# Attention kernel, last ten units: PV ten slots behind to the end, sums turned by DMA up to unit 125, closing tiles finished one after the other, tail loads spread over six units

## The chip, the cores and the metric

The kernel runs on one core of one Trainium2 chip. A core has five engines that run side by side, each with its own instruction stream in fixed order: TensorE (PE, matrix products into PSUM), VectorE (DVE), ScalarE (ACT, here the exponentials), GpSimd (POOL) and SyncE (SP). DMAs are issued from the streams of SP, POOL and ACT. The metric is the device time of one execution in microseconds (us); lower is better. Three runs of the kernel before gave 1253.02, 1253.81 and 1254.78 us; the median is 1253.81.

## The reference

Sizes: 2048 tokens, D = 512, 32 heads of 128, 2048 cached keys, MLP width 1792. All inputs are bf16. `mixer_mlp` stands for the second branch, a token mixer and an MLP with two GELUs.

```
def _A_ref(x, k_cache, v_cache, wq, wo):
    q = (x @ wq).reshape(B, Sq, H, Dh).transpose(0, 2, 1, 3)
    scores = einsum("bhqd,bhkd->bhqk", q, k_cache) * (Dh ** -0.5)
    p = softmax(scores, axis=-1)
    o = einsum("bhqk,bhkd->bhqd", p, v_cache)
    return o.transpose(0, 2, 1, 3).reshape(B, Sq, H * Dh) @ wo

xn = layernorm(x)
s = _A_ref(xn, k_cache, v_cache, wq, wo)
g = silu(mixer_mlp(xn, w1, w2, w3, w4))
return x + s * g
```

## The kernel before, in words

**Units and slots.** The attention is cut into 128 units (`units`, L130): 8 groups of 4 heads, in each group 4 query tiles of 512 tokens, in each of these the 4 heads. A unit has 8 slots, p0 to p7, 1024 slots in all (the loop of L791). In each slot PE forms the scores of 256 keys (`s_slot`, 2 matmuls into one of two PSUM buffers `ps_s`), ACT takes the exponential into `pT` (L207, 128x1024), and PE multiplies earlier exponentials with the values (`pv_slot`, 2 matmuls into `ps_o`, two buffers). How many slots PV runs behind the scores is read from the list `LAGS` (L137): 5 at the start, 10 from the middle of unit 6 on, and between unit 120 and p2 of unit 122 back to 5, one at a time, so that five slots there hold two PV pairs.

**Other work in the slots.** PE also forms the next queries (`q_mm`, 4 matmuls in p0 and p1 of a unit, none in the last two units), the products with `wo` for one tile of 128 tokens (`wo_mm`, p4 and p5; DVE adds the result to `s_acc` in p6, `wo_post`) and the matmuls of the second branch (`ps_m`, p2, p3, p6, p7), which end in unit 120. Of the two single PSUM buffers, `xa` and `xm`, `wo` uses `xa` and the second branch `xm`.

**The sum of the softmax.** DVE adds the exponentials of a unit (`add_first`, `add_next`, `fold`) to one tile of 128x512; what is left is a sum over the 128 partitions. There are two ways. For *turned* units (`turned`, L249: units 4 to 117, `T1` = 118) SP issues a DMA transpose of the tile into `accT` (`acc_turn`, p3 of the next unit), DVE reduces it (`turned_sums`, L260, at p0 of the unit after that), takes the reciprocal (L245), SP writes it to DRAM (`dr`) and reads it back spread over all partitions (`rb`, `bcast`, p2), and DVE normalises `ps_o` with it into `oT` (`norm`, L287, p7, two units later). There is one buffer `accT` and one `rb`. For the other units PE forms the sum with 4 matmuls on a column of ones (`sums`, L240, p3 of the next unit), the rest is the same, `bcast` comes one slot later and `norm` (L294) at p2 of the unit after.

**The end.** `QUIET` is unit 121. The products of the last two query tiles with the heads of group 6 are deferred: their `oT` goes to DRAM (`o_d`) and is loaded back as `oS` by `tail_open` at the start of unit 121, with the gates `gf` and inputs `xf` of token tiles 12 to 15 (10 loads in one place of the program). Tiles 8 to 11 belong to query tile 2 of the last group; the loop finishes 8, 9 and 10, each with 4 matmuls on `oS` and 4 on `oT`. DVE writes each out (`wo_out`, p3 of the next unit). `gate_sum` (L332, L334) prepares the sums of tiles 12 to 15. After the loop (L888 on) come the sum of unit 127 in three pieces (`split_sums`, 40 small matmuls), its last five PV slots, tile 11, then tiles 12 to 15: the parts that need only heads 0 to 2 first, then `norm` of unit 127 in two halves, then head 3 of tiles 12 and 13, tile 14, and tile 15 in two halves. `last_scale` (L338, DVE) and `last_out` (L343, on POOL for tiles 12 and 13, on DVE for the rest) end each tile.

Of the kernel before, what the change touches and what calls it, by code (L numbers as in the profile page):

```python
# [10 lines left out]
FP32 = mybir.dt.float32  # L11
BF16 = mybir.dt.bfloat16
# [5 lines left out]
def kernel(  # L18
# [15 lines left out]
    nc = tc.nc  # L34
# [9 lines left out]
    NT = Sq // P  # L44
# [180 lines left out]
    def pv_slot(u, p):  # L225
        g, qt, hh = units[u]
        s = st[u]
        if p == 0:
            s["o"] = psO.tile([P, 512], FP32, name="ps_o")
        pT = s["pT"][p // 2]  # L230
        for j in range(2):
            kc = 2 * p + j
            mm(s["o"][:], vBs[g * HG + hh][:, kc, :], pT[:, 2 * (p % 2) + j, :], kc == 0, kc == KC - 1)

    def sums(u):
        s = st[u]
        ps = psX.tile([P, 4], FP32, tag="xm" if u + 1 == QUIET - 1 else "xa", name="ps_sum")
# [11 lines left out]
    def turned(u):  # L249
        return T0 <= u < T1  # L250
# [22 lines left out]
            recip(s, s["ps"])  # L273

    def bcast(u):
        st[u]["rb"] = rp.tile([P, 512], FP32, name="rb")
        pin(nc.sync.dma_start(
            out=st[u]["rb"][:], in_=st[u]["dr"][:].rearrange("a b -> (a b)").partition_broadcast(P)))

    def norm(u, pieces=1):  # L280
        g, qt, hh = units[u]
        s = st.pop(u)
        if hh == 0:
            oTs[(g, qt)] = otp.tile([P, HG, 512], BF16, name="oT")
        if turned(u):
            f = "x (j p) -> x j p"
            pin(nc.vector.tensor_tensor(  # L287
                out=oTs[(g, qt)][:, hh, :].rearrange(f, j=4), in0=s["o"].rearrange(f, j=4),
                in1=s["rb"].rearrange("x (p j) -> x j p", j=4), op=ALU.mult))
            return  # L290
        w = 512 // pieces
        for i in range(pieces):
            c = slice(i * w, (i + 1) * w)
            pin(nc.vector.tensor_tensor(  # L294
                out=oTs[(g, qt)][:, hh, c], in0=s["o"][:, c], in1=s["rb"][:, c], op=ALU.mult))

    wo_box = {}

    def wo_mm(g, t, hhs, tag="xa"):
        if hhs[0] == 0:  # L300
            wo_box[0] = psX.tile([P, D], FP32, tag=tag, name="ps_wo")
        held = g == NG - 1 and (NG - 2, t // 4) in deferred
        if held and hhs[0] == 0:
            wo_part(wo_box[0][:], g - 1, t, range(HG), True, False)
        wo_part(wo_box[0][:], g, t, hhs, hhs[0] == 0 and not held, hhs[-1] == HG - 1)
# [10 lines left out]
    def tail_open():  # L316
        ph.close()
        ph3 = ph.enter_context(pool("ph3", reuse_waits="tile"))
        for g, qt in deferred:
            oTs[(g, qt)] = ph3.tile([P, HG, 512], BF16, name=f"oS{qt}")  # L320
            pin(nc.sync.dma_start(out=oTs[(g, qt)][:], in_=o_d[qt][:]))
        for t in range(4 * LQ, NT):
            gf = ph3.tile([P, D], BF16, name=f"gf{t}")
            pin(nc.sync.dma_start(out=gf[:], in_=g_d[t][:]))
            xf = ph3.tile([P, D], BF16, name=f"xf{t}")
            pin(nc.sync.dma_start(out=xf[:], in_=xsrc[t]))
            tl[t] = (gf, xf)

    def gate_sum(t):
        gf, xf = tl[t]  # L330
# [10 lines left out]
    def last_out(t, eng, cs=slice(0, D), queue=nc.sync):  # L341
        gf, xf = tl[t]
        pin(eng.tensor_tensor(out=xf[:, cs], in0=gf[:, cs], in1=s_acc[:, t, cs], op=ALU.add))  # L343
        pin(queue.dma_start(out=out2d[t * P:(t + 1) * P, cs], in_=xf[:, cs]))
# [10 lines left out]
    def wo_post(g, t):  # L355
        ps = wo_box.pop(0)
        sa = s_acc[:, t, :]
        if g == 0:
            pin(nc.vector.tensor_copy(out=sa, in_=ps[:]))
            return  # L360
        pin(nc.vector.tensor_tensor(out=sa, in0=ps[:], in1=sa, op=ALU.add))  # L361

    def wo_out(t):
        sa = s_acc[:, t, :]
        xl, gl = fin.pop(t)
        pin(nc.vector.scalar_tensor_tensor(
            out=gl[:], in0=sa, scalar=0.5, in1=gl[:], op0=ALU.mult, op1=ALU.mult))
        pin(nc.vector.tensor_tensor(out=xl[:], in0=gl[:], in1=xl[:], op=ALU.add))
        pin(nc.sync.dma_start(out=out2d[t * P:(t + 1) * P, :], in_=xl[:]))
# [421 lines left out]
    for n in range(NS):  # L791
# [33 lines left out]
            acc_turn(u - 1)  # L825
        if p == 2 and u >= 2 and turned(u - 2):
            bcast(u - 2)
        if p == (4 if u == T1 + 2 else 2) and u >= 2 and not turned(u - 2):
            normed(u - 2)
        if p == 3 and u >= 1 and not turned(u - 1):  # L830
            sums(u - 1)
        if p == 4 and u >= 1 and u != T1 + 1 and not turned(u - 1):
# [12 lines left out]
        if u == QUIET - 1 and p >= 6:  # L845
            wo_mm(*wo_todo[0], (0, 1) if p == 6 else (2, 3), "xm")
            if p == 7:
                gg, t = wo_todo.popleft()
                wo_post(gg, t)
                at(n + 5, lambda t=t: wo_out(t))  # L850
        if p == 4:
            add_first(u)
        if p == 4 and u == NU - 1:
# [37 lines left out]
    assert min(todo) >= NS and not chunks and len(wo_todo) == 1  # L891
    U = NU - 1
    GL = NG - 1
    s = st[U]
    gg, t11 = wo_todo.popleft()
    ts = [4 * LQ + j for j in range(4)]
    norm(U - 1)
    held = range(HG)
    ready = range(HG - 1)
    pv_slot(U, 3)  # L900
    split_sums(U, [(s["acc"][:, i, :], i == 0, False) for i in range(2)]
               + [(s["pT"][2][:, i, :], False, False) for i in range(4)])
    pv_slot(U, 4)
    split_sums(U, [(s["pT"][3][:, i, :], False, False) for i in range(2)])
    pv_slot(U, 5)
    split_sums(U, [(s["pT"][3][:, i, :], False, i == 3) for i in range(2, 4)])
    bcast(U)
    for fn in late:
        fn()
    for t in ts[2:]:  # L910
        gate_sum(t)
    pv_slot(U, 6)
    pv_slot(U, 7)
    wo_mm(gg, t11, (0, 1, 2, 3))
    wo_post(gg, t11)
    wo_out(t11)
# [5 lines left out]
    for j in (0, 1):  # L922
        wo_part(dst[j], GL - 1, ts[j], held, True, False)
        wo_part(dst[j], GL, ts[j], ready, False, False)
    wo_part(dst[2], GL - 1, ts[2], held, True, False)
    norm(U, 2)
    for j in (0, 1):
        wo_part(dst[j], GL, ts[j], (HG - 1,), False, True)
        last_scale(ts[j], dst[j])
        last_out(ts[j], nc.gpsimd)  # L930
    wo_part(dst[2], GL, ts[2], range(HG), False, True)
    last_scale(ts[2], dst[2])
    last_out(ts[2], nc.vector)
    for i, queue in enumerate((nc.sync, nc.scalar)):
        cs = slice(i * D // 2, (i + 1) * D // 2)
        ps = halves[i][:, cs]
        wo_part(ps, GL - 1, ts[3], held, True, False, cs)
# [34 lines left out]
```

## Time and profile before

| | |
|---|---|
| time, median of 3 runs | 1253.81 us |
| the profiled execution: its time | 1253.69 us |
| its span in the trace | 1251.9 us |
| PE / DVE / ACT / POOL busy | 1242.8 / 1107.5 / 1130.6 / 139.5 us |
| exponentials (L207) | 1024 of 1028 ns mean |
| DMA moved | 126.70 MB |

The span is counted from the first to the last record of the profiled execution; the rest of its time, 1.8 us, lies around it. Times in the profile are microseconds from the start of the span. A matmul's record holds its passage through the array, so records of matmuls that follow each other overlap, and the distance of their starts is what one costs; the same holds, less so, for DVE. L123 is the helper that issues every matmul, so PE work is told apart by the tile it writes. PEld is the load of a matmul's weights, which overlaps the matmul before. In square brackets a row shows how long the engine sat idle before it and what ended that.

### The profile page before, as it was taken

The page shows a single profiled execution, that of the slowest core. Times are in us where ns is not written, and L with a number is a line of the kernel's source. Part 1 is how long each engine was busy: PE and PEld are TensorE (multiplying, and loading weights), DVE is VectorE, ACT ScalarE, POOL GpSimd, SP SyncE. Part 2 cuts the span into 40 slices and gives each one's busy share as a digit, 9 for nine tenths or more (in the row PEclk, how much of TensorE's full clock was granted, in tenths as well). Part 3 has the DMA queues.
Part 4 walks back from the last instruction along what each step waited for, and adds up shares of the span by engine and source line. Part 5 has one row for each costly group of instructions (what it writes and reads, how often), then busy time and mean ns, then how long its engine had stood idle before and what let it go on. Part 6 is the DMA issues. An engine that isn't in the chain of part 4 may idle for free.

```text
span 1251.9 us, 16586 instructions
## 1 busy us (share of the span) xinstructions
PE 1242.8 (99%) x5872; PEld 599.1 (48%) x5872; DVE 1107.5 (88%) x1509; ACT 1130.6 (90%) x1285; POOL 139.5 (11%) x239
## 2 busy tenths in 40 slices
PE   9999999999999999999999999999999999999998
PEld 5444444444444444444444444444444444444444
DVE  7899999999899988899988889999888999888887
ACT  7999998888999888899988889998888999988893
POOL 4410003332101000000100000010000000000111
PEclk9999999999999999999999999999999999999999
DMA  9654444565635555344663345554535343564532
GB/s 185 136 114 88 78 106 80 118 149 109 135 72 114 118 95 102 61 91 90 111 126 76 69 93 97 110 71 108 97 89 108 66 89 81 115 134 74 154 72 69
DMA packets 235108, 126.70 MB, mean 101 GB/s; under 512 B 186832, under 2 KB 212048, under 8 KB 235024
## 3 DMA queue, kind: packets, MB, share of 16 engines
q1 hardware_dynamic: 225920, 100.40, 41.8%
q0 software_dynamic: 8672, 24.91, 7.9%
q8 instruction: 46, 0.75, 0.3%
q14 instruction: 38, 0.31, 0.1%
q10 hardware_dynamic: 432, 0.33, 0.1%
HBM read 82.58 MB, written 7.60 MB: 72 GB/s over the span
## 4 chain that ended last, share of the span: by engine, by line
PE 96%; DMA 1%; ACT 1%; DVE 1%; issue 0%; SPq 0%; POOL 0%; POOLq 0%; DVEq 0%
PE ps_s L123 35%; PE ps_o L123 34%; PE ps_m L123 10%; PE ps_q L123 9%; PE ps_wo L123 8%; ACT pT L207 1%; DMA dr<-rc 1%; DMA w_sb<-in_B_w_dram 0%; DMA rb<-dr 0%; PE ps_sum L123 0%; DVE gf L338 0%; DVE xf L343 0%; ACT pre L528 0%; DVE qT L193 0%; DVE bn L384 0%
## 5 line engine op out<-in xcount | busy, mean ns | idle before, releaser
L207 ACT ACTIVATE pT<-ps_s 128x1024 bf16<-128x1024 f32 x1024 | 1024.4, 1028 | 99.2 <-PE ps_s L123 88.7
L123 PE MATMUL ps_s<-qT,kT 128*128 128x512 bf16 x2048 | 608.9, 379 | 0.9 <-ACT pT L207 0.5
L123 PE MATMUL ps_o<-pT,vb 128*128 128x512 bf16 x2048 | 608.0, 379 | 0.3 <-DVE oT L294 0.3
L123 PEld LDWEIGHTS <-kT 128*128 128x128 bf16 x2048 | 231.1, 113 | 226.1 <-issue 4.9
L218 DVE TENSOR_TENSOR acc<-acc,pT 128x2048 bf16<-128x2048 bf16 x254 | 306.4, 1206 | 10.1 <-ACT pT L207 9.9
L123 PEld LDWEIGHTS <-vb 128*128 128x128 bf16 x2048 | 200.0, 98 | 225.8 <-DMA vb<-in_A_v_cache_dram 0.5
L213 DVE TENSOR_TENSOR acc<-pT 128x2048 bf16<-128x2048 bf16 x128 | 156.2, 1220 | 31.8 <-ACT pT L207 31.6
L123 PE MATMUL ps_q<-xnT,wq_h 128*128 128x512 bf16 (+1 forms) x524 | 152.8, 374 | 0.8 <-ACT xnT L459 0.6
L123 PE MATMUL ps_wo<-wo_h,oT 128*128 128x512 bf16 (+1 forms) x476 | 140.2, 377 | 0.2 <-DVE qT L193 0.2
L287 DVE TENSOR_TENSOR oT<-ps_o,rb 128x512 bf16<-128x512 f32 x114 | 122.3, 1073 | 8.9 <-DMA rb<-dr 8.9
L361 DVE TENSOR_TENSOR s_acc<-ps_wo,s_acc 128x512 f32<-128x512 f32 x100 | 68.7, 687 | 43.5 <-PE ps_wo L123 43.2
L222 DVE TENSOR_TENSOR acc<-acc 128x1024 bf16<-128x1024 bf16 x127 | 86.8, 683 | 0.9
L193 DVE CAST qT<-ps_q 128x512 bf16<-128x512 f32 x109 | 74.9, 688 | 8.7 <-PE ps_q L123 7.7
L123 PEld LDWEIGHTS <-wq_h 128*128 128x128 bf16 x524 | 50.8, 98 | 61.1 <-issue 1.3
L260 DVE TENSOR_REDUCE sm<-accT 128x4 f32<-128x512 bf16 x114 | 77.5, 680 | 0.5 <-DMA accT<-acc 0.2
L123 PE MATMUL ps_m<-xn2T,w_sb 128*128 128x512 bf16 x224 | 77.1, 379 | 0.0
L123 PE MATMUL ps_m<-w_sb,h2T 128*128 128x512 bf16 x224 | 77.1, 379 | 0.0
L123 PEld LDWEIGHTS <-oT 128*128 128x128 bf16 x484 | 47.3, 98 | 57.6 <-DVE oT L294 1.4
L659 POOL DMA_DIRECT2D w_sb<-in_B_w_dram x28 | 21.1, 754 | 370.4 <-PE ps_m L123 370.4
L687 POOL DMA_DIRECT2D g_d<-xr x16 | 8.7, 546 | 442.3 <-DVE xr L685 376.5
L223 DVE TENSOR_TENSOR acc<-acc 128x512 bf16<-128x512 bf16 x127 | 54.0, 425 | 4.4
L496 DVE SCALAR_TENSOR_TENSOR sq<-sq,pre 128x1024 bf16<-128x1024 bf16 x36 | 44.0, 1221 | 3.9 <-ACT sq L492 3.9
(89 smaller groups left out, 602.9 us busy)
## 6 DMA issues: line engine op xcount, KB each, us to landing
rb<-dr SPq DMA_DIRECT2D x128, 256.0 KB, 4.2
vb<-in_A_v_cache_dram SPq DMA_DIRECT2D x64, 256.0 KB, 3.6
w_sb<-in_B_w_dram POOLq DMA_DIRECT2D x28, 256.0 KB, 3.8
wo_h<-in_A_wo_dram SPq DMA_DIRECT2D x32, 128.0 KB, 3.0
wq_h<-in_A_wq_dram SPq DMA_DIRECT2D x28, 128.0 KB, 3.1
kT<-in_A_k_cache_dram SPq DMA_TRANSPOSE x128, 3.4
dr<-rc SPq DMA_DIRECT2D x128, 2.0 KB, 1.6
xr<-in_A_x_dram POOLq DMA_DIRECT2D x16, 128.0 KB, 2.5
```

The lines of the kernel that those rows point to most:

```text
L123: pin(nc.tensor.matmul(out=out, lhsT=lhsT, rhs=rhs, start=start, stop=stop))
L193: pin(nc.vector.tensor_copy(out=qT[:], in_=st[u].pop("psq")[:]))
L207: pin(nc.scalar.activation(out=s["pT"][-1][:, jj:jj + 2, :], in_=sps[:], func=ACT.Exp, scale=SCALE))
L213: pin(nc.vector.tensor_tensor(out=s["acc"][:], in0=s["pT"][0][:], in1=s["pT"][1][:], op=ALU.add))
L218: pin(nc.vector.tensor_tensor(out=a[:], in0=a[:], in1=st[u]["pT"][i][:], op=ALU.add))
L222: pin(nc.vector.tensor_tensor(out=a[:, 0:2, :], in0=a[:, 0:2, :], in1=a[:, 2:4, :], op=ALU.add))
L223: pin(nc.vector.tensor_tensor(out=a[:, 0, :], in0=a[:, 0, :], in1=a[:, 1, :], op=ALU.add))
L260: pin(nc.vector.tensor_reduce(out=sm[:], in_=s.pop("at")[:], axis=mybir.AxisListType.X, op=ALU.add))
L287: pin(nc.vector.tensor_tensor(out=oTs[(g, qt)][:, hh, :].rearrange(f, j=4), in0=s["o"].rearrange(f, j=4), in1=s["rb"].rearrange("x (p j) - ...
L361: pin(nc.vector.tensor_tensor(out=sa, in0=ps[:], in1=sa, op=ALU.add))
L496: pin(nc.vector.scalar_tensor_tensor(out=sq[:].rearrange(f2), in0=sq[:].rearrange(f2), scalar=1.0, in1=pre[:].rearrange(f2), op0=ALU.add, ...
L659: pin(nc.gpsimd.dma_start(out=w[:], in_=w3_v[:, :, fc * P:(fc + 2) * P]))
```

## The change

- `LAGS` no longer goes down: PV stays 10 slots behind to the end, so 10 PV slots are left after the loop instead of 5 (6 and 7 of unit 126, all of 127).
- `T1` is 126: units 118 to 125 are turned too, 126 and 127 are summed on PE. In unit 127 `sums` and `bcast` of unit 126 come one slot later than before. The special places of `bcast` and `normed` around the old `T1` go. `rb` of units 126 and 127 gets two buffers of its own.
- The loads of the tail are issued one group per unit at p5 of units 121 to 126, in the order: `gf`, `xf` of tile 12; of 13; `oS` of query tile 2; `gf`, `xf` of 14; `oS` of 3; `gf`, `xf` of 15.
- The wo products: `normed` of unit 123 now falls in p7 of unit 125, so tile 8 is done in unit 126, tile 9 in 127 (their parts on `oS` in p2 and p3, on `oT` in p4 and p5, in `xm`); tiles 10 and 11 are left for after the loop. The second wo tile of unit 120 (`QUIET` - 1, p6 and p7) goes; tiles 3 to 7 are then done one per unit in 121 to 125.
- After the loop: the sums of unit 127, with PV slots 6 and 7 of unit 126 between them, then tile 10, the eight PV slots of unit 127, tile 11, then tiles 12, 13, 14 whole, each with its scale and its add, and 15 in halves. All adds of `last_out` are on DVE.

```diff
-    T0, T1 = 4, NU - 10
-    LAGS = [(T0 * SPU + 4 * (i + 1), LAG + i) for i in range(5)] + [((T1 + 2) * SPU + 2, LAG + 5)]
-    LAGS += [((T1 + 2) * SPU + 6 + 4 * i, LAG + 4 - i) for i in range(4)] + [(NS, LAG)]
+    T0, T1 = 4, NU - 2
+    LAGS = [(T0 * SPU + 4 * (i + 1), LAG + i) for i in range(5)] + [(NS, LAG + 5)]
...
-        st[u]["rb"] = rp.tile([P, 512], FP32, name="rb")
+        st[u]["rb"] = (tl["rb"].tile([P, 512], FP32, tag="rb3", bufs=2, name="rb") if u >= T1 else rp.tile([P, 512], FP32, name="rb"))
...
+    def held_load(g, qt):
+        pin(nc.sync.dma_start(out=oTs[(g, qt)][:], in_=o_d[qt][:]))
+
+    def gate_load(t):
+        for tile_, src in zip(tl[t], (g_d[t][:], xsrc[t])):
+            pin(nc.sync.dma_start(out=tile_[:], in_=src))
...
+    loads = [lambda t=t: gate_load(t) for t in range(4 * LQ, NT)]
+    for i, (g, qt) in enumerate(deferred):
+        loads.insert(2 + 2 * i, lambda g=g, qt=qt: held_load(g, qt))
+    for i, load in enumerate(loads):
+        at((QUIET + i) * SPU + 5, load)
...
-        if p == 3 and u >= 1 and not turned(u - 1):
+        if p == (4 if u > T1 else 3) and u >= 1 and not turned(u - 1):
             sums(u - 1)
...
         if p in (4, 5) and wo_todo:
-            wo_mm(*wo_todo[0], (0, 1) if p == 4 else (2, 3))
+            wo_mm(*wo_todo[0], (0, 1) if p == 4 else (2, 3), "xm" if u >= NU - 2 else "xa")
+        if p in (2, 3) and u >= NU - 2:
+            wo_held(*wo_todo[0], (0, 1) if p == 2 else (2, 3))
...
+    split_sums(U, [(a, i == 0, False) for i, a in enumerate(acc + pT2)])
+    pv_slot(U - 1, 6)
+    split_sums(U, [(a, False, False) for a in pT3[:2]])
+    pv_slot(U - 1, 7)
+    split_sums(U, [(a, False, i == 1) for i, a in enumerate(pT3[2:])])
     bcast(U)
     for fn in late:
         fn()
     for t in ts[2:]:
         gate_sum(t)
+    norm(U - 1)
+    while wo_todo:
+        gg, t = wo_todo.popleft()
+        wo_mm(gg, t, range(HG), "xa" if wo_todo else "xm")
+        wo_post(gg, t)
+        if wo_todo:
+            fin_load(t + 1)
+        wo_out(t)
+        if wo_todo:
+            for p in range(SPU):
+                pv_slot(U, p)
+            norm(U, 2)
...
+    for j in range(3):
+        wo_part(dst[j], GL - 1, ts[j], range(HG), True, False)
+        wo_part(dst[j], GL, ts[j], range(HG), False, True)
         last_scale(ts[j], dst[j])
-        last_out(ts[j], nc.gpsimd)
-    wo_part(dst[2], GL, ts[2], range(HG), False, True)
-    last_scale(ts[2], dst[2])
-    last_out(ts[2], nc.vector)
+        last_out(ts[j], nc.vector)
```

More of the change, by code (lines that the diff above doesn't have):

```diff
@@ L236, in sums @@
         s = st[u]
-        ps = psX.tile([P, 4], FP32, tag="xm" if u + 1 == QUIET - 1 else "xa", name="ps_sum")
+        ps = psX.tile([P, 4], FP32, tag="xa", name="ps_sum")
         a = s["acc"][:, 0, :].rearrange("k (p j) -> k j p", j=4)
@@ L299, in wo_mm, with wo_held @@
     def wo_mm(g, t, hhs, tag="xa"):
+        held = g == NG - 1 and (NG - 2, t // 4) in deferred
+        if held and 0 not in wo_box:
+            wo_held(g, t, range(HG), tag)
+        if hhs[0] == 0 and not held:
+            wo_box[0] = psX.tile([P, D], FP32, tag=tag, name="ps_wo")
+        wo_part(wo_box[0][:], g, t, hhs, hhs[0] == 0 and not held, hhs[-1] == HG - 1)
+    def wo_held(g, t, hhs, tag="xm"):
         if hhs[0] == 0:
             wo_box[0] = psX.tile([P, D], FP32, tag=tag, name="ps_wo")
[L302 to L305, printed above, removed]
+        wo_part(wo_box[0][:], g - 1, t, hhs, hhs[0] == 0, False)
     def wo_part(ps, g, t, hhs, first, last, cs=slice(0, D)):
@@ L318, in tail_open @@
         ph3 = ph.enter_context(pool("ph3", reuse_waits="tile"))
+        tl["rb"] = ph3
         for g, qt in deferred:
             oTs[(g, qt)] = ph3.tile([P, HG, 512], BF16, name=f"oS{qt}")
-            pin(nc.sync.dma_start(out=oTs[(g, qt)][:], in_=o_d[qt][:]))
         for t in range(4 * LQ, NT):
[L323 to L327, printed above, removed]
+            tl[t] = [ph3.tile([P, D], BF16, name=f"{name}{t}") for name in ("gf", "xf")]
+    def held_load(g, qt):
[3 more added lines that the diff above has]
+            pin(nc.sync.dma_start(out=tile_[:], in_=src))
     def gate_sum(t):
@@ L827 @@
             bcast(u - 2)
-        if p == (4 if u == T1 + 2 else 2) and u >= 2 and not turned(u - 2):
+        if p == 2 and u >= 2 and not turned(u - 2):
             normed(u - 2)
-        if p == 3 and u >= 1 and not turned(u - 1):
+        if p == (4 if u > T1 else 3) and u >= 1 and not turned(u - 1):
             sums(u - 1)
-        if p == 4 and u >= 1 and u != T1 + 1 and not turned(u - 1):
+        if p == (5 if u > T1 else 4) and u >= 1 and not turned(u - 1):
             bcast(u - 1)
         if p in (4, 5) and wo_todo:
-            wo_mm(*wo_todo[0], (0, 1) if p == 4 else (2, 3))
+            wo_mm(*wo_todo[0], (0, 1) if p == 4 else (2, 3), "xm" if u >= NU - 2 else "xa")
+        if p in (2, 3) and u >= NU - 2:
+            wo_held(*wo_todo[0], (0, 1) if p == 2 else (2, 3))
         if p == 6 and QUIET <= u < NU - 1:
@@ L890 @@
     late = [fn for n in sorted(todo) for fn in todo[n]]
-    assert min(todo) >= NS and not chunks and len(wo_todo) == 1
+    assert min(todo) >= NS and not chunks and len(wo_todo) == 2
     U = NU - 1
@@ L894 @@
     s = st[U]
-    gg, t11 = wo_todo.popleft()
     ts = [4 * LQ + j for j in range(4)]
[L897 to L906, printed above, removed]
+    acc = [s["acc"][:, i, :] for i in range(2)]
+    pT2, pT3 = ([s["pT"][i][:, j, :] for j in range(4)] for i in (2, 3))
+    split_sums(U, [(a, i == 0, False) for i, a in enumerate(acc + pT2)])
[3 more added lines that the diff above has]
+    split_sums(U, [(a, False, i == 1) for i, a in enumerate(pT3[2:])])
     bcast(U)
@@ L936 @@
         ps = halves[i][:, cs]
-        wo_part(ps, GL - 1, ts[3], held, True, False, cs)
+        wo_part(ps, GL - 1, ts[3], range(HG), True, False, cs)
         wo_part(ps, GL, ts[3], range(HG), False, True, cs)
```

20 lines of the change are left out of this document (removed).

## The prediction

> **What bounds the kernel now.** I read the page's first part, then the windows of the last 60 us, then the chain of waits from its end backwards, then the timelines of single engines.
>
> ```profile
> span 1251.9 us, 16586 instructions
> PE 1242.8 (99%) x5872; PEld 599.1 (48%) x5872; DVE 1107.5 (88%) x1509; ACT 1130.6 (90%) x1285; POOL 139.5 (11%) x239
> ...
> 1190.00:1200.00 10.00, 10.00 (x52) 4.80 (x50) 8.49 (x13) 9.19 (x11) 1.08 (x2) 1.00 0.35 86
> 1235.00:1240.00 5.00, 5.00 (x47) 2.71 (x45) 3.81 (x8) 0.00 (x0) 0.00 (x0) 1.00 0.04 5
> 1240.00:1245.00 5.00, 4.60 (x22) 1.94 (x21) 4.10 (x8) 0.00 (x0) 0.17 (x1) 1.00 0.38 105
> 1245.00:1252.00 7.00, 1.84 (x17) 1.40 (x15) 4.14 (x7) 0.00 (x0) 2.11 (x2) 0.81 0.23 75
> ```
>
> The columns of a window are its length, then PE, PEld, DVE, ACT, POOL, granted clock, DMA share, GB/s. PE is full up to 1240, at full clock (1.00). What it does there can be moved within the stretch for nothing, so only two things shorten the end: less PE work, and less time in which PE stands or is already done. The chain shows the second:
>
> ```profile
> 1236.98 2.64 DMA dr<-rc
> 1239.69 3.43 DMA rb<-dr
> 1243.14 0.44 DVE oT L294
> ...
> 1245.97 1.68 DVE xf L343
> ...
> 1248.82 0.42 DVE xf L343
> ```
>
> The columns are start, length, what. The sum of unit 127 goes out and back (6.16 us, 1236.98 to 1243.14), then DVE normalises, and DVE ends the path at 1249.24. On PE and POOL at that place:
>
> ```profile
> 1242.20 1.03 PE L123 MATMUL ps_wo<-wo_h,oS 128*128 128x512 bf16 x4
> 1243.63 0.61 PE L123 MATMUL ps_s<-wo_h,oT 128*128 128x512 bf16 x2 [0.40 <-DVE oT L294]
> 1246.24 0.60 PE L123 MATMUL ps_wo<-wo_h,oT 128*128 128x256 bf16 x4
> ...
> 1236.88 0.69 DVE L366 SCALAR_TENSOR_TENSOR gl<-s_acc,gl 128x512 bf16<-128x512 f32 x1
> 1242.04 0.43 DVE L368 TENSOR_TENSOR xl<-gl,xl 128x512 bf16<-128x512 bf16 x1
> 1245.26 0.68 DVE L338 SCALAR_TENSOR_TENSOR gf<-ps_wo,gf 128x512 bf16<-128x512 f32 x1
> 1247.58 0.41 DVE L338 SCALAR_TENSOR_TENSOR gf<-ps_wo,gf 128x256 bf16<-128x256 f32 x1
> 1248.37 0.42 DVE L338 SCALAR_TENSOR_TENSOR gf<-ps_wo,gf 128x256 bf16<-128x256 f32 x1
> ...
> 1244.83 2.27 POOL L343 TENSOR_TENSOR xf<-gf,s_acc 128x512 bf16<-128x512 bf16 x2 [19.08 <-DVE gf L338]
> ```
>
> Now the rows of an ordinary unit near the end, with the cost of the sums on PE:
>
> ```profile
> 1193.13 0.27 PE L123 MATMUL ps_sum<-ones_t,acc 128*128 128x1 bf16 x4
> 1193.27 0.60 PE L123 MATMUL ps_s<-qT,kT 128*128 128x512 bf16 x2
> 1193.70 0.59 PE L123 MATMUL ps_o<-pT,vb 128*128 128x512 bf16 x2
> 1201.94 0.27 PE L123 MATMUL ps_sum<-ones_t,acc 128*128 128x1 bf16 x4
> ...
> 1196.55 4.02 ACT L207 ACTIVATE pT<-ps_s 128x1024 bf16<-128x1024 f32 x4 [0.25 <-PE ps_s L123]
> 1200.85 1.02 ACT L207 ACTIVATE pT<-ps_s 128x1024 bf16<-128x1024 f32 x1 [0.27 <-PE ps_s L123]
> ```
>
> From start to start two big matmuls take 0.43 (1193.27 to 1193.70), one 0.216; four small ones take 0.14. The unit lasts 8.81 (1193.13 to 1201.94) for 40 big matmuls (16 scores, 16 PV, 4 queries, 4 wo), which need 8.63, and the four small ones. ACT idles only 0.25 + 0.27 in it: PE leads, ACT is close behind.
>
> **The change part by part.**
>
> *Sums of units 118 to 125 leave PE.* 8 x 0.14 = 1.1 us less PE work. ACT's 0.5 of idle per unit says that most of it comes through, but two exponentials' buffers couple the engines slot by slot, and some 0.03 per unit may turn into a wait for ACT. I take -0.9; bounds -1.1 and -0.4 (half the units held by ACT).
>
> *What they put on DVE and SP.* Each adds a transpose and a reduction, and a slower `norm` (L287 in place of L294). A turned unit from a stretch where PE is as full:
>
> ```profile
> 1132.52 0.18 DVE L245 RECIPROCAL rc<-sm 128x4 f32<-128x4 f32 x1
> ...
> 1139.28 1.07 DVE L287 TENSOR_TENSOR oT<-ps_o,rb 128x512 bf16<-128x512 f32 x1
> 1140.27 0.67 DVE L260 TENSOR_REDUCE sm<-accT 128x4 f32<-128x512 bf16 x1
> 1140.98 0.18 DVE L245 RECIPROCAL rc<-sm 128x4 f32<-128x4 f32 x1
> ...
> 1132.72 0.32 SPq L247 DMA_DIRECT2D dr<-rc  x1
> 1134.61 0.32 SPq L277 DMA_DIRECT2D rb<-dr  x1
> 1135.52 1.19 SPq L255 DMA_TRANSPOSE accT<-acc  x1
> ...
> DMA to landing us min/median/max: 3.4/4.3/5.7
> ```
>
> (The last row is `rb`, last 150 us.) From start to start L287 to L260 is 0.99, L260 to L245 0.71. Against that the DVE of a unit near the end, not turned:
>
> ```profile
> 1193.44 0.18 DVE L245 RECIPROCAL rc<-ps_sum 128x4 f32<-128x4 f32 x1 [0.47 <-PE ps_sum L123]
> ...
> 1196.33 1.22 DVE L218 TENSOR_TENSOR acc<-acc,pT 128x2048 bf16<-128x2048 bf16 x1 [0.54 <-ACT pT L207]
> 1198.52 1.23 DVE L218 TENSOR_TENSOR acc<-acc,pT 128x2048 bf16<-128x2048 bf16 x1 [0.36 <-ACT pT L207]
> 1200.85 0.68 DVE L294 TENSOR_TENSOR oT<-ps_o,rb 128x512 bf16<-128x512 f32 x1
> 1202.25 0.18 DVE L245 RECIPROCAL rc<-ps_sum 128x4 f32<-128x4 f32 x1 [0.72 <-PE ps_sum L123]
> 1211.05 0.18 DVE L245 RECIPROCAL rc<-ps_sum 128x4 f32<-128x4 f32 x1 [0.46 <-PE ps_sum L123]
> ```
>
> Of the 8.81 from 1193.44 to 1202.25 DVE stood 0.54 + 0.36 + 0.72 = 1.6; it worked 7.2. Turned it works 0.99 - 0.68 + 0.71 = 1.0 more: 8.2 of the 8.6 that a unit will last. In units 122 and 124, with a `gate_sum`, it stood only 0.46 (to 1211.05) and worked 8.3; with 1.0 more it runs 0.7 over, and gives back 0.4 in the unit between, so about 1.0 late at most. What waits for DVE on PE is the first PV of a unit, into the `ps_o` that `norm` empties. `norm` stands behind the wo addition of p6 and starts about 0.5 into the next unit, ends at 1.5, and PE wants the buffer at p2, 3.0 in (p0 and p1 of six matmuls, then two). 1.5 of cover, so I cost this at nothing. Without it each us late is a us lost.
>
> The Trainium skill speaks against this step: "VectorE: DVE Perf Modes", Rules for kernel authors, says that a tensor reduction runs at single rate, is the slowest DVE operation, and that one on a hot path should be restructured. The rate agrees with the trace as far as rows can show (0.67 for 512 elements). By that rule, with DVE as the bound, eight units would cost 8 x 1.0 = 8 us instead of nothing; by the idle time above DVE isn't yet the bound.
>
> *The loop through the DMAs.* With one `rb` and the reduction behind `norm` on DVE, each unit's chain is `norm` 0.99, L260 0.71, L245 0.2, `dr` to the issue of `rb` 1.9 (1132.72 to 1134.61), `rb` 4.3: 8.1 of 8.6. The quoted unit went round in 8.46 (1132.52 to 1140.98) with no wait marked ahead of L287, shorter than the coming units. Cost nothing; bound for the range below, with slower transfers. On SP the queue is `dr`, `rb`, the transpose, the output of a tile, then the loads at p5; a load holds `dr` of the next unit only by its issue, three slots earlier. The loads land units before they are used: `oS` of query tile 2 is issued in unit 123 and first read in 126.
>
> *PV ten behind to the end, and tiles 8 to 11 a unit later.* Ten PV matmuls (2.2 us) and eight wo matmuls (1.7) move from inside the loop to after it. PE is full in both places, so the sum is zero. ACT covers it: it must do its units in 8.6, and needs 8.81 - 0.52 = 8.3. Without that cover up to 0.3 per unit would be lost. The wo products now fill p2 and p3 of units 126 and 127 and shorten runs of four-matmul slots in which PE is held by ACT: -0.1 (bounds 0 and -0.2).
>
> *The wait for the last sum.* PE is through with tile 14's deferred part at 1242.20 + 4 x 0.216 = 1243.06 and starts again at 1243.63: 0.57. After the change the sums end with tile 10 (1.73), eight PV slots (3.45), tile 11 (1.73) and seven matmuls of tile 12 (1.51) still ahead: 8.4 us of PE work, against 0.3 for the reciprocal, 6.16 for the trip and 0.44 for `norm`, 6.9. In front of `norm` of unit 127 DVE has in that time the output of tile 9, two `gate_sum`s, `norm` of unit 126 and tile 10: the stretch from 1236.88 to 1242.47, which holds one output, the two `gate_sum`s and tile 11, took 5.6, and a `norm` is 0.7 more. The wait goes: -0.57, bounds -0.57 and 0 (a trip 1.5 slower).
>
> *Behind the last matmul.* PE issues its last at 1246.24 + 4 x 0.108 = 1246.67, DVE ends at 1249.24: 2.57. The delay is tile 14's add of 1.68, next to POOL's 2.27 for tiles 12 and 13; the same add on tile 15 takes 0.42 for half the width, after POOL is done. With POOL out and tiles 12 and 13 finished while PE is at the next one (1.1 of DVE in 1.73 of PE), what follows is tile 14's scale and add (0.71, 1245.26 to 1245.97, + 0.42), 0.2 after its matmuls, and two halves of 0.79 (1247.58 to 1248.37), with 1.73 of PE between: the end is 1.2 after the last issue. -1.35, bounds -0.9 and -1.5. The last transfer (2.7, 1249.24 to 1251.9) stays.
>
> Sum: -0.9 - 0.1 - 0.57 - 1.35 = -2.9; the profiled execution's own 1253.69 becomes 1250.8. It lies 0.1 under the median of the runs shown (1253.81), and 1250.8 is 0.24% under that.
>
> **The rivals.**
>
> 1. *ACT takes the place of the sums, and the trip stays on the path.* For it: ACT's 0.5 of idle. Against: the waits before its exponentials name PE. The upper bounds of these terms: -0.4 - 0 - 0 - 1.35 = -1.75: 1251.9.
>
> 2. *Slower: the loop through the DMAs is too long.* Place: L287 of units 119 to 124, then PE's first `ps_o`. If `rb` takes its 5.7 instead of 4.3 and `dr` its 2.6, the chain is 10.2, 1.6 more than a unit, in six units 9.6, less the 1.5 of cover: 8.1 of stall, less 2.9: 1258.9. It decides from a trip of 6.7 us (`dr` and `rb` together) on; 6.2 was typical. For it: the loads now run among transposes. Against: the quoted unit.
>
> 3. *It does no more than drop PE work, and fully* (the better case): no coupling with ACT, -1.1 - 0.2 - 0.57 - 1.5 = -3.4: 1250.3.
>
> **How the numbers follow.** A measurement of this kernel can tell about 0.2%, 2.5 us, from no change: faster is below 1251.3, slower above 1256.3. My forecast gets 0.52 (own range 1250.2 to 1251.8; of it 0.42 faster, 0.10 same), rival 1 0.20 (0.18 same, 0.02 faster), rival 2 0.20 (0.18 slower, 0.02 same, where the loop is only a little too long), rival 3 0.08 (faster). Faster 0.52, same 0.30, slower 0.18. The range reaches from 1249.6, a little under rival 3, to 1255.5, the mild end of rival 2.
>
> **What would show it.** Right: PE's last matmul ends about 1.5 us earlier and no idle time is marked ahead of it; DVE's last add comes 1.2 after; units 122 to 125 last 8.65 to 8.7; L343 takes 0.4 each. Wrong: waits of `ps_o` for L287, or of L287 for `rb`, in units 119 to 126 (rival 2); PE slots of four matmuls at 0.9 where the sums were, or PE still waiting for `norm` of unit 127 (rival 1).

## The result, and the profile after

The changed kernel takes 1252.13 us, median of 22 runs (1250.62 to 1253.25), against 1253.57 for the kernel before, median of as many. The ratio is 0.9987, with a 95% interval of 0.9982 to 0.9993: faster by 0.13%, which is 1.6 us; the medians are 1.4 us apart. That is about half of the 2.9 that were forecast. The time lies outside the forecast's own range, 1250.2 to 1251.8, and above the 1251.3 from which the prediction would have called it faster. The profiled execution of the changed kernel took 1252.74.

The first lines of its page. DVE is busy 7.8 us more, about what the eight turned sums were to cost (8 x 1.0). PE has 147 fewer records, of which the change explains the 32 matmuls of eight sums; the rest are records missing from the trace, so PE's sums are not compared:

```profile
span 1251.0 us, 16420 instructions
PE 1235.6 (99%) x5725; PEld 598.5 (48%) x5840; DVE 1115.3 (89%) x1519; ACT 1130.3 (90%) x1285; POOL 137.4 (11%) x237
```

Where the time went is read best by cutting the last 100 us in two at a row which every version has: the start of the last exponential. First the timeline of ACT before, then after (lines of the changed kernel below the edits are shifted; the exponential, L207, is L206 now, L287 is L286, L294 is L293, L338 is L345, L343 is L350):

```profile
1148.07 3.12 ACT L207 ACTIVATE pT<-ps_s 128x1024 bf16<-128x1024 f32 x3 [0.33 <-PE ps_s L123]
...
1232.95 1.94 ACT L207 ACTIVATE pT<-ps_s 128x1024 bf16<-128x1024 f32 x2 [0.33 <-PE ps_s L123]
```

```profile
1148.41 3.12 ACT L206 ACTIVATE pT<-ps_s 128x1024 bf16<-128x1024 f32 x3 [0.33 <-PE ps_s L123]
...
1229.51 1.94 ACT L206 ACTIVATE pT<-ps_s 128x1024 bf16<-128x1024 f32 x2 [0.33 <-PE ps_s L123]
```

The third exponential of the upper rows is the first of unit 119; the second of the lower rows is the last of all. The changed kernel is 0.34 late at the upper rows already, in a stretch where both programs are the same: the change has no part in that. With the start of each exponential taken one by one, the stretch from unit 119 to the last exponential ("loop") and from there to the end of the span ("tail") lasted, in us:

| profile of | loop | tail | sum |
|---|---|---|---|
| before | 83.70 | 18.05 | 101.75 |
| forecast: 3.9 of PE work moved behind the loop, -1.0 in the loop, -1.92 in the tail | 78.8 | 20.0 | 98.8 |
| after | 79.92 | 20.54 | 100.46 |

So 1.1 of the shortfall lies in the loop and 0.5 in the tail.

The loop first. Units 122 to 124 last 8.76, not 8.65 to 8.7, and in units 125 and 126, which last 9.31 and 9.08, PE stands. From PE's timeline (first slot of units 124 and 125, then the stalled pairs of PV), DVE's and SP's:

```profile
1194.53 0.59 PE L123 MATMUL ps_s<-qT,kT 128*128 128x512 bf16 x2
...
1203.29 0.59 PE L123 MATMUL ps_s<-qT,kT 128*128 128x512 bf16 x2
...
1206.95 0.59 PE L123 MATMUL ps_o<-pT,vb 128*128 128x512 bf16 x2 [0.70 <-DVE oT L286]
...
1214.43 0.59 PE L123 MATMUL ps_s<-qT,kT 128*128 128x512 bf16 x2
1215.17 0.59 PE L123 MATMUL ps_o<-pT,vb 128*128 128x512 bf16 x2
...
1195.85 1.06 DVE L286 TENSOR_TENSOR oT<-ps_o,rb 128x512 bf16<-128x512 f32 x1
1205.84 1.06 DVE L286 TENSOR_TENSOR oT<-ps_o,rb 128x512 bf16<-128x512 f32 x1 [0.56 <-DMA rb<-dr]
1214.05 1.07 DVE L286 TENSOR_TENSOR oT<-ps_o,rb 128x512 bf16<-128x512 f32 x1
...
1199.95 0.32 SPq L276 DMA_DIRECT2D rb<-dr  x1
```

`rb` is issued at 1199.95 and lands 5.9 later, where 4.3 was typical; `norm` starts 9.99 after the one before it, in units of 8.76; the first PV matmul of the next unit waits 0.70 for the `ps_o` that `norm` empties. The windows of the changed kernel around that place (columns as in the prediction):

```profile
1190.00:1200.00 10.00, 9.95 (x47) 4.75 (x46) 9.69 (x15) 9.38 (x12) 1.08 (x2) 1.00 0.58 145
1200.00:1210.00 10.00, 9.30 (x44) 4.42 (x44) 9.27 (x15) 9.33 (x11) 1.08 (x2) 1.00 0.69 104
```

PE falls from 9.95 to 9.30, and DVE, at 8.49 before in the first of these windows, stands at 9.69. The second stall shows in PE's rows as a gap: 0.74 from the `ps_s` at 1214.43 to the `ps_o`, where 0.43 is normal. No transfer is late there: `norm` (1214.05) has no wait marked ahead of it and starts 8.21 after the one before. PE, which has no queries to form in unit 126, is back for the buffer sooner, 7.91 after the last time (1206.95 to 1214.86). The first stall is the sign of rival 2, at a mild price; the second is DVE still behind with its work, in a unit where PE leaves it less time.

The tail, from the chain of waits and the timelines of PE and DVE:

```profile
1233.09 2.99 DMA dr<-rc
1236.13 3.95 DMA rb<-dr
1240.18 0.16 DVE oT L293
...
1247.86 0.42 DVE xf L350
```

```profile
1246.10 0.60 PE L123 MATMUL ps_wo<-wo_h,oT 128*128 128x256 bf16 x4
...
1242.29 0.42 DVE L375 TENSOR_TENSOR xl<-gl,xl 128x512 bf16<-128x512 bf16 x1
...
1246.01 0.69 DVE L350 TENSOR_TENSOR xf<-gf,s_acc 128x512 bf16<-128x512 bf16 x1
1247.07 0.42 DVE L350 TENSOR_TENSOR xf<-gf,s_acc 128x256 bf16<-128x256 bf16 x1
```

PE now goes through without a mark of idle time, as forecast: the 0.57 is gone. Its last issue is at 1246.10 + 4 x 0.108 = 1246.53, and DVE ends at 1248.28, 1.75 after it. Before it was 2.57; the forecast was 1.2. Two things are in the difference. A full-width add takes 0.69. And the trip of the last sum took 7.1 (1233.09 to 1240.18), where 6.16 was forecast, so that `norm` of unit 127 came late, and from then on the chain runs on DVE alone.

### The profile page after: what moved, and what is told of

Its sections match the earlier page's. It is cut to its first block, busy times and chain, and to the rows that moved or that the text cites. A ratio compares the mean times of both kernels' runs of the same rounds, so it can differ in the third digit from the quotient of the medians.

```text
span 1251.0 us, 16420 instructions
## 1 busy us (share of the span) xinstructions
PE 1235.6 (99%) x5725; PEld 598.5 (48%) x5840; DVE 1115.3 (89%) x1519; ACT 1130.3 (90%) x1285; POOL 137.4 (11%) x237
## 4 chain that ended last, share of the span: by engine, by line
PE 88%; DVE 5%; DMA 4%; issue 1%; ACT 1%; POOL 0%; SPq 0%; DVEq 0%; POOLq 0%
PE ps_o L123 32%; PE ps_s L123 31%; PE ps_m L123 10%; PE ps_q L123 8%; PE ps_wo L123 7%; DMA rb<-dr 2%; DVE acc L217 1%; DMA dr<-rc 1%; DMA xin<-in_A_x_dram 1%; DVE acc L212 1%; DVE oT L286 1%; ACT pT L206 1%; DVE sm L259 0%; DMA kT<-in_A_k_cache_dram 0%; DVE gl L373 0%
## 5 line engine op out<-in xcount | busy, mean ns | idle before, releaser
L206 ACT ACTIVATE pT<-ps_s 128x1024 bf16<-128x1024 f32 x1024 | 1024.0, 1028 | 96.0 <-PE ps_s L123 80.0
L123 PE MATMUL ps_o<-pT,vb 128*128 128x512 bf16 x2015 | 600.8, 379 | 5.2 <-DMA vb<-in_A_v_cache_dram 0.8
L123 PE MATMUL ps_s<-qT,kT 128*128 128x512 bf16 x1992 | 596.9, 379 | 2.4 <-ACT pT L206 0.5
L286 DVE TENSOR_TENSOR oT<-ps_o,rb 128x512 bf16<-128x512 f32 x122 | 130.8, 1072 | 9.4 <-DMA rb<-dr 9.4
L259 DVE TENSOR_REDUCE sm<-accT 128x4 f32<-128x512 bf16 x122 | 82.9, 680 | 0.0
```

Of the source, the lines that this page charges most:

```text
L123: pin(nc.tensor.matmul(out=out, lhsT=lhsT, rhs=rhs, start=start, stop=stop))
L206: pin(nc.scalar.activation(out=s["pT"][-1][:, jj:jj + 2, :], in_=sps[:], func=ACT.Exp, scale=SCALE))
L259: pin(nc.vector.tensor_reduce(out=sm[:], in_=s.pop("at")[:], axis=mybir.AxisListType.X, op=ALU.add))
L286: pin(nc.vector.tensor_tensor(out=oTs[(g, qt)][:, hh, :].rearrange(f, j=4), in0=s["o"].rearrange(f, j=4), in1=s["rb"].rearrange("x (p j) - ...
```

## The experiments

Ratios are to the kernel before on the same chip. One theory runs through all: the loop through the DMAs costs the changed kernel about 1 us in stalls of PV, ACT takes most of what the sums would bring, and the tail's gain comes from finishing the tiles in turn.

**a0_again: the changed kernel once more.** No edit.

> The changed kernel once more, unaltered, to see which of its waits come back. Profile of after: PE stands 0.65 us at 1206.30 and 0.31 at 1214.86 before a first PV matmul, because the normalisation of unit 121 came behind an rb that took 5.86 us to land (4.0 is the median). Theory 'late rb by chance': the stall moves to another unit or is gone, and the span varies by about 1 us with it. Theory 'DVE and the chain are too long in units 122 to 125': both stalls are there again, at the same units and of about the same size. Time against the kernel before: 0.9987 again, within 0.001.

1251.72 (1250.56 to 1253.93), ratio 0.9981 [0.9971, 0.9990]; loop 80.31, tail 20.27. PE's stalls, then DVE ahead of the first, then the end:

```profile
1189.77 0.59 PE L123 MATMUL ps_o<-pT,vb 128*128 128x512 bf16 x2 [0.82 <-DVE oT L286]
1207.34 0.59 PE L123 MATMUL ps_o<-pT,vb 128*128 128x512 bf16 x2 [0.20 <-DVE oT L286]
...
1178.43 1.07 DVE L286 TENSOR_TENSOR oT<-ps_o,rb 128x512 bf16<-128x512 f32 x1 [0.65 <-DMA rb<-dr]
1180.29 0.69 DVE L259 TENSOR_REDUCE sm<-accT 128x4 f32<-128x512 bf16 x1 [0.79 <-DMA accT<-acc]
...
1246.49 0.60 PE L123 MATMUL ps_wo<-wo_h,oT 128*128 128x256 bf16 x4
1247.96 0.43 DVE L350 TENSOR_TENSOR xf<-gf,s_acc 128x256 bf16<-128x256 bf16 x1
```

The two marked stalls, 1.0 together, lie in other units than before: here a late transpose (0.79) makes the sum late and the next `norm` with it. In unit 126 PE stands 0.3 again (from the `ps_s` at 1214.82 to the `ps_o` at 1215.55 it is 0.73). So the loss belongs to the kernel: the part in unit 126 comes back, and the place of the rest is decided by which transfer happens to be slow. The tail has no late trip this time (1233.48 to 1239.64, 6.16): DVE ends 1.47 after PE's last issue (1246.92 to 1248.39). The forecast of -1.35 meant 1.22; that leaves 0.25 to the width of the add, and 0.28 to the trip in the first profile.

**e1_sums_on_pe: units 118 to 125 summed on PE again**, all else as changed.

```
-        return T0 <= u < T1
+        return T0 <= u < NU - 10
```

> The change without its second part: units 118 to 125 are summed on PE again (four small matmuls at p3, normalisation at p2 two units later), all else as changed. The prediction's price (PE leads, four small matmuls are 0.14 us, 8 units): 1.1 us more PE work, less the stalls of about 1.0 that turning brought, so about the same as the changed kernel, and units 122 to 124 last 8.90 us (8.76 + 0.14). Theory 'ACT holds PE anyway': the units last 8.81 as before the change (0.05 more, not 0.14), the stalls before PV are gone, and the kernel is 0.5 us faster than the changed one, about 0.9983 of before.

1252.50 (1252.20 to 1255.52), ratio 0.9992 [0.9983, 1.0000]; loop 80.23, tail 20.25. PE's timeline:

```profile
1164.70 0.27 PE L123 MATMUL ps_sum<-ones_t,acc 128*128 128x1 bf16 x4 [0.37 <-DVE qT L192]
...
1196.47 0.59 PE L123 MATMUL ps_q<-xnT,wq_h 128*128 128x512 bf16 x2
1205.28 0.59 PE L123 MATMUL ps_q<-xnT,wq_h 128*128 128x512 bf16 x2
```

Its unit lasts 8.81 (1196.47 to 1205.28), against 8.76 in the changed kernel (1194.53 to 1203.29): four small matmuls are worth 0.05, not 0.14. It has no stall of PV, but one of the sums themselves behind DVE in unit 120, which lasts 9.45 where 8.79 is normal. The two kernels' intervals overlap; the 0.5 us by which this one was expected to be faster than the changed kernel did not come. With the sums on PE the loop is as long as with the trips (79.92 and 80.31), and the whole time from unit 119 on is the same too (100.48, against 100.46 and 100.57). So the turned sums, less what their trips cost, bring nothing that these runs can tell from zero; the gain over the kernel before lies in the other parts of the change.

**e2_no_trip: the turned sums without the read of `rb`** (units 118 to 125 are normalised with an old `rb`, so the write and the reduction stay and nobody waits for the spread).

```
+        if NU - 10 <= u < T1:
+            st[u]["rb"] = rb_kept[0]
+            return
```

> The changed kernel with the trip of rb left out for units 118 to 125: they are normalised with the rb of unit 117, and the eight reads of dr are not issued. Transposes, reductions and the rest stay. Theory 'the trip sets the stalls': no wait of DVE for rb before unit 126 and no stall of PE before PV; units 122 to 125 last 8.76, last exponential 1.0 us earlier than in the changed kernel's profile. Rival 'DVE is too full by itself': PE still stands before PV in units 123 to 126, by 0.3 us or more in all.

One run, 1250.75; loop 79.06, tail 20.26. PE's timeline has no marked idle time ahead of a PV, and the unit is

```profile
1194.53 0.60 PE L123 MATMUL ps_q<-xnT,wq_h 128*128 128x512 bf16 x2
1203.29 0.60 PE L123 MATMUL ps_q<-xnT,wq_h 128*128 128x512 bf16 x2
```

8.76 all the same. The loop is 0.86 shorter than in the changed kernel's first profile and 1.25 shorter than in its second: that is the price of waiting for the trip, measured against one profile, in which the eight reads are also gone from the DMA engines. Against before it is 4.64 shorter, where the forecast had 4.9; the matmuls that moved cost nothing.

**e3_no_qcopy: ACT without its share of the query copies** (from unit 123 on the copy of `ps_q` to `qT` is left out and old queries are used; the matmuls stay).

```
+        if u > QUIET + 1:
+            st[u].pop("psq")
+            st[u]["qT"] = st[u - 1]["qT"]
+            return
```

> The changed kernel without the copies of the queries on ACT for units 123 to 127 (those units use the queries of unit 122): ACT has 0.5 us less to do in each of units 121 to 125, PE's work is unchanged. Theory 'ACT took the place of the sums': the 0.09 us that PE stands before the second scores behind p4 goes, and units 121 to 124 last 8.63 to 8.68 instead of 8.76. Rival 'something on PE itself costs it' (weight loads, matmuls that change buffers): they last 8.76 as before.

One run, 1251.03; loop 79.01. PE's timeline:

```profile
1194.58 0.59 PE L123 MATMUL ps_q<-xnT,wq_h 128*128 128x512 bf16 x2
1203.25 0.59 PE L123 MATMUL ps_q<-xnT,wq_h 128*128 128x512 bf16 x2
```

8.67, against 8.63 of matmuls (40 x 0.216). The sums' missing 0.09 was ACT: in the changed kernel the scores of p5 wait for an exponential that stands behind the query copy. The place in the changed kernel, on PE and on ACT:

```profile
1199.71 0.59 PE L123 MATMUL ps_wo<-wo_h,oT 128*128 128x512 bf16 x2
1200.23 0.59 PE L123 MATMUL ps_s<-qT,kT 128*128 128x512 bf16 x2
...
1198.67 0.59 ACT L190 ACTIVATE qT<-ps_q 128x512 bf16<-128x512 f32 x1
```

The scores start 0.52 after the products with `wo`, where two matmuls take 0.43. In this run DVE waits for `rb` only once, 0.17 in unit 122; still units 125 and 126 last 8.74 and 9.09, so unit 126 stalls without a slow trip just ahead of it. The loop is as short as in e2 for another reason, and the two can't be added.

**e4_adds_on_dve: the kernel before, with only the adds of `last_out` moved to DVE.**

```
-        last_out(ts[j], nc.gpsimd)
+        last_out(ts[j], nc.vector)
```

> The kernel before with one edit: the last adds of tiles 12 and 13 on DVE instead of POOL. The prediction held that tile 14's add took 1.68 us because POOL worked beside it, and that an add of 128x512 is 0.42. Theory 'beside POOL': tile 14's add takes 0.69 (what it takes in the changed kernel). The end: DVE has two adds of 0.69 more behind the normalisation and 1.0 less at tile 14, so its last add ends 0.3 to 0.5 us later than 1249.24 if it is DVE's own work that sets the end. Rival 'POOL was the delay, moving its work alone brings the gain': it ends 0.5 us or more earlier.

One run, 1253.61; loop 83.69, tail 18.26 against 18.05. The end of its chain of waits:

```profile
1246.86 0.69 DVE xf L343
...
1248.71 0.42 DVE xf L343
```

POOL out by itself brings nothing. Tile 14's add takes 0.69 here, not 1.68: as the prediction held, POOL's work beside it had made it slow. But DVE now does the two other adds as well, so that from the start of `norm` to the last add it takes 6.56 (1242.57 to 1249.13) instead of 6.10. It does five scales and five adds one after the other, beginning at `norm` of unit 127. By this reading the gain needs the tiles finished in turn behind an earlier `norm`; that part was not tried by itself.

**e5_loads_at_once: the tail's loads in one place again**, p5 of unit 121.

```
-        at((QUIET + i) * SPU + 5, load)
+        at(QUIET * SPU + 5, load)
```

> The changed kernel with its ten tail loads issued at one place again (p5 of unit 121) instead of over six units. Theory 'the loads slow the trips': in units 121 and 122 dr or rb land later than 2.5 and 4.5 us, the normalisation of unit 120 comes late and PE stands before PV in unit 122 or 123; from unit 123 on rb lands in about 4.0 and there is no stall. Rival 'spreading is not what matters': the stalls and the landing times are as in the changed kernel.

One run, 1253.72; loop 82.51. SP, DVE and PE:

```profile
1180.52 0.39 SPq L246 DMA_DIRECT2D dr<-rc  x1
1185.58 0.32 SPq L276 DMA_DIRECT2D rb<-dr  x1
...
1189.11 1.05 DVE L286 TENSOR_TENSOR oT<-ps_o,rb 128x512 bf16<-128x512 f32 x1 [1.97 <-DMA rb<-dr]
...
1190.20 0.59 PE L123 MATMUL ps_o<-pT,vb 128*128 128x512 bf16 x2 [2.58 <-DVE oT L286]
1208.20 0.59 PE L123 MATMUL ps_o<-pT,vb 128*128 128x512 bf16 x2 [0.63 <-DVE oT L286]
```

`dr`, 2 KB, is issued behind the last load and takes 5.06 until `rb` can follow (1180.52 to 1185.58); PE loses 3.2 in two places. Spreading the loads is not decoration: with turned sums it is worth 2.2 to 2.6 us of loop, by this one profile.

**v1_turn_to_119: turned sums for 118 and 119 alone.**

```
-        return T0 <= u < T1
+        return T0 <= u < NU - 8
```

> The changed kernel with turning up to unit 119 only: units 120 to 125 are summed on PE. In the profiles so far four small matmuls cost 0.05 us in a unit of this stretch (8.81 against 8.76), the stalls before PV came in units 123 to 126 and cost 0.9 to 1.2 us together, and the one stall that PE sums brought (0.37, in unit 120, behind the copy of a query) was for the sum of unit 119. Theory 'the chain through rb costs more than the sums': six units of 8.81, no PE wait for a normalisation before unit 127, the last exponential 0.7 us earlier than in the two profiles of the changed kernel (taken from unit 119 on), about 0.9976 of before. Rival 'the sums on PE cost their full 0.14': units of 8.90, 0.8 us in all, and the time of the changed kernel.

1254.10 (1253.07 to 1256.38), ratio 1.0001 [0.9992, 1.0009]; loop 81.36, tail 20.13. The later units are free of stalls, but the passage from turned units to others is not. PE's timeline:

```profile
1175.36 0.29 PE L123 MATMUL ps_sum<-ones_t,acc 128*128 128x1 bf16 x4 [0.98 <-DVE acc L222]
1185.96 0.59 PE L123 MATMUL ps_wo<-wo_h,oT 128*128 128x512 bf16 x2 [0.61 <-DVE rc L244]
```

Two units of 9.97 and 9.57 take 2 us more than two of 8.76. In them DVE has a turned sum and a sum on PE at once. The special places of `bcast` and `normed`, which the change dropped, may have spread that before; no run tried them here. The theory, which expected a ratio of 0.9976, missed this.

**v2_tile11_first: v1 with tiles 10 and 11 both ahead of the PV of unit 127.**

```
-        if wo_todo:
-            for p in range(SPU):
-                pv_slot(U, p)
-            norm(U, 2)
+    for p in range(SPU):
+        pv_slot(U, p)
+    norm(U, 2)
```

(The added lines stand behind the loop over the tiles.)

> The same as v1_turn_to_119, and after the loop tile 11 is done before the PV slots of unit 127 instead of after them, so that its addition and output (1.8 us of DVE) no longer stand behind the normalisation of unit 127. Theory 'DVE behind the last trip sets the end': DVE's last add comes up to 0.3 us earlier counted from the last exponential, no more, because PE's own end (last matmul, then 1.5 of DVE) is that close behind. Rival 'the trip still sets the end': no gain, DVE waits for rb and PE for the normalisation. Against v1: 0 to 0.3 us, below what five rounds can tell; the trace decides.

1254.98 (1253.83 to 1255.94), ratio 1.0008 [0.9998, 1.0017]; tail 20.75 against 20.13 of v1. PE now waits for the last `norm`:

```profile
1243.19 0.39 PE L123 MATMUL ps_s<-wo_h,oT 128*128 128x512 bf16 x1 [0.44 <-DVE oT L293]
```

So tile 11 behind the PV is cover that the trip needs; the changed kernel's order is the better one.

**v3_loads_on_pool: the loads issued from POOL instead of SP.**

```
-            pin(nc.sync.dma_start(out=tile_[:], in_=src))
+            pin(nc.gpsimd.dma_start(out=tile_[:], in_=src))
```

(the same in `held_load`)

> The changed kernel with its ten tail loads issued by POOL instead of SP, at the same places. With all loads at one place on SP, dr of the next unit took 5.04 us to land behind them and PE stood 2.58 before PV. Theory 'dr and rb queue behind the loads of their own queue': with the loads on another queue dr lands in 1.4 to 1.7 us in units 122 to 126 (1.67 to 2.48 in the changed kernel), rb in about 4.0, the stalls before PV of about 1.0 us go, ratio about 0.9973. Rival 'the transfers share the DMA engines, whatever the queue': dr and rb land as before, stalls of 0.5 to 1.2 us in all remain, ratio as the changed kernel's, 0.998 to 0.9987.

1255.23 (1252.73 to 1257.75), ratio 1.0011 [1.0002, 1.0020]; loop 81.07, tail 20.74. PE's stalls, POOL's and SP's issues and DVE behind them:

```profile
1188.68 0.59 PE L123 MATMUL ps_o<-pT,vb 128*128 128x512 bf16 x2 [0.36 <-DVE oT L286]
1207.20 0.59 PE L123 MATMUL ps_o<-pT,vb 128*128 128x512 bf16 x2 [0.94 <-DVE oT L286]
1215.68 0.59 PE L123 MATMUL ps_o<-pT,vb 128*128 128x512 bf16 x2 [0.41 <-DVE oT L286]
...
1198.12 0.53 POOL L330 DMA_DIRECT2D oS<-o_d  x1
1199.20 0.32 SPq L276 DMA_DIRECT2D rb<-dr  x1
1206.10 1.05 DVE L286 TENSOR_TENSOR oT<-ps_o,rb 128x512 bf16<-128x512 f32 x1 [0.76 <-DMA rb<-dr]
```

`rb`, on SP's queue with `oS` on POOL's just ahead, takes 6.9 (1199.20 to 1206.10). Another queue does not take the loads out of the way. The Trainium skill says so in "DMA: Bandwidth & Descriptors", Issuing engines are not separate DMA queues: whichever engine starts them, transfers run on the same 16 DMA engines and interleave. This run agrees: its stalls before PV are 1.7 us, and its loop is 0.8 to 1.2 us longer than in the two profiles of the changed kernel, not shorter.

**v4_sum_before_norm: the reduction ahead of `norm` on DVE for units 119 to 125** (p7 of the next unit instead of p0 of the one after).

```
-        if p == 0 and u >= 2 and turned(u - 2):
+        if p == 0 and u >= 2 and turned(u - 2) and u - 2 < QUIET - 2:
             turned_sums(u - 2)
...
+        if p == SPU - 1 and turned(u - 1) and u - 1 >= QUIET - 2:
+            turned_sums(u - 1)
```

> The changed kernel with two DVE steps exchanged in units 120 to 126: the reduction of the next unit's sum and its reciprocal (0.8 us) stand ahead of the normalisation of the unit before, not behind it. The trip of a sum then starts about 1.0 us earlier against the place where its rb is needed, and the normalisation comes 0.8 later where rb is in time. Theory 'the trip behind the normalisation sets the stalls': a landing of 5.9 us no longer reaches PE; no stall before PV above 0.2 us; last exponential 1.0 us earlier (from unit 119 on) than in the two profiles of the changed kernel; ratio about 0.9973. Rival 'DVE is too full, any order': the normalisation, 0.8 later, makes PE stand in most units from 122 on, and the ratio rises to 0.999 or more.

1252.32 (1251.50 to 1254.32), ratio 0.9985 [0.9976, 0.9994]; loop 79.54, tail 20.25. The window of this kernel from 1200 to 1210, then DVE's order in it:

```profile
1200.00:1210.00 10.00, 10.00 (x47) 4.66 (x46) 9.83 (x15) 9.38 (x12) 1.08 (x2) 1.00 0.40 107
...
1205.40 0.68 DVE L259 TENSOR_REDUCE sm<-accT 128x4 f32<-128x512 bf16 x1
...
1206.21 1.05 DVE L286 TENSOR_TENSOR oT<-ps_o,rb 128x512 bf16<-128x512 f32 x1
```

The sum goes out before `norm` and the trip gains its 0.99. PE is full in the window, where it had 9.30 in the changed kernel, with more work done on DVE (9.83 against 9.27). No `norm` of the loop up to unit 126 waits for `rb` any more. The loop is 0.38 and 0.77 shorter than in the two profiles of the changed kernel, where 1.0 was expected, and 0.48 longer than in e2: units 121, 123 and 125 last 8.80 to 8.82, and unit 126 lasts 9.08 (from the `ps_s` at 1214.79 to the `ps_o` at 1215.53 it is 0.74). With no wait for `rb` left, that rest fits what the new order itself costs, a `norm` that stands 0.8 later on DVE.

The profile from unit 119 on is 0.67 and 0.79 shorter than in the two profiles of the changed kernel, but the timed runs can't tell it from the changed kernel (0.9985 and 0.9981, each with 0.0009 on either side). No version that keeps all the work was shown to be faster than the changed kernel.

## Why the prediction was right in sign and half in size

1. **Sums off PE, -0.9: mis-sized.** The place where ACT takes over was named ("some 0.03 per unit may turn into a wait for ACT"), but it takes 0.09 of the 0.14 in the steady units: 8.81, 8.76 and 8.67 in e1, the changed kernel and e3. The idle time of ACT, 0.5 per unit, was read as slack; it lies in other slots than the one where the query copy delays the exponential for which p5 waits. The lower bound, -0.4, was near: without the trip the whole loop is 0.26 short of the forecast.

2. **The loop through the DMAs, costed at nothing: the step that failed.** It costs 0.86 in the first profile and 1.25 in the second, measured against e2. Two numbers of that step were wrong. The cover of 1.5 was counted from a `norm` that starts 0.5 into its unit. In e2, without a wait for `rb`, the one of unit 124 starts 0.75 in; in the changed kernel it starts 1.32 in (1194.53 to 1195.85), because DVE waited 0.48 for `rb` in unit 122 and, at 9.7 of 10 us, had not made that up. It ends 2.4 in, and PE wants the buffer 2.96 in (1203.29 to 1206.25): 0.6 is left. And the trip was taken at its median, 6.2, while a slow one, 2.2 and 5.9 for `rb` (1197.75 to 1205.81), uses up that rest. The lateness of DVE and the slow trip had each been held against the whole of the 1.5, and never against it together. Rival 2 was right in mechanism and place for the stalls before unit 126: a round of 9.99 decided, in one unit of the first profile instead of six, since the next trips were normal again. The 0.31 of unit 126 comes back in the second profile, and in e3, e5 and v4 (9.08 or 9.09 against 8.77 in e2); there the `norm` waits for DVE's earlier work and not for `rb` (point 3).

3. **DVE, costed at nothing: its work was sized well, the cover that it leaves was not.** In e2 it takes 8.21 from `norm` to `norm` in a unit without a `gate_sum` and 9.35 in one with it; the forecast was 8.2 and 9.3. The Trainium skill's warning on reductions did not come true as a price of 8 us: e2 keeps all of them and shows no stall, v4 keeps them too and loses 0.48 to e2. But a DVE that is nearly full keeps a `norm` late that has once become late. In unit 126, which has no queries, it shows: PE comes back for the buffer after 7.91 us, DVE after 8.21. The prediction took its 3.0 us before the first PV from units with queries.

4. **PV ten behind and tiles a unit later: right.** The loop became shorter and the tail longer by the moved work; e2's loop is 4.64 shorter of 4.9, its tail 2.21 longer of 1.98.

5. **The wait for the last sum, -0.57: right.** PE doesn't stand in any run with the changed order; v2 shows that tile 11 behind the PV is part of the cover.

6. **Behind the last matmul, -1.35: mis-sized.** -0.82 in the first profile, -1.10 in the second. The full-width add was costed with 0.42, the price of the same add at half width. It takes 0.69 (0.25 at the end); one operand, `s_acc`, is f32, and the add of the same width without one takes 0.42 (L375). The forecast chain held otherwise. The other 0.28 was a trip of 7.1 instead of 6.16. That the engine of the adds alone does not bring this gain, e4 shows; that finishing in turn does is what remains, and was not tried alone.

Added up for the first profile: -2.92, + 0.26 (1), + 0.86 (2 and 3), + 0.25 + 0.28 (6) = -1.27, with 101.75 - 100.46 = 1.29 measured; the 0.34 from before unit 119 leaves 0.95 of 1253.69 - 1252.74. What that 0.34 is stays open; the second profile has it as well, e2's has 0.54 the other way at that place with the same program up to it, and over all profiles the start of unit 119 lies anywhere between 1149.17 and 1152.15. That is why single profiles are compared from there on.

The measured 1252.13 lies next to rival 1's 1251.9, but that is luck. Of rival 1, ACT took the place of the sums, while the trip of the last sum did leave PE's path; the stalls of the loop, which rival 1 does not have, and the tail's 0.5 make up the rest.

## What to carry to other kernels

A loop of engine work and transfers must be held against its slowest trip, not the median one, and the cover counted from where the waiting instruction really starts on an engine that the same change fills. When small work leaves the fullest engine, look in which slot the second engine is late, not at its idle time over the unit. Price an instruction by a row with the same operands and the same width: the type shown first is not always the one that sets its time.

## What the runs showed of the hardware

- A full-width add of two bf16 tiles took 0.42 (L375) and the same shape with an f32 tile as second operand 0.69 (L350), though both rows read "128x512 bf16<-128x512 bf16".
- A 256 KB spread read (`rb`), 4.3 in the median and 5.7 at most in the last 150 us of the kernel before, took 5.9 next to loads of the same queue and 6.9 next to a load from POOL's (v3).
- An add of 128x512 on DVE took 1.68 while POOL did two adds of the same form in 2.27, and 0.69 when POOL did none (L343 before and in e4).
- A 2 KB write behind a run of loads on its queue took 5.06 until its reader could be issued (e5), against 1.9 in the prediction's rows.
